# Attention and a gated product on one Trainium2 core: value rows issued from ScalarE's queue, queries of two groups by one set of transfers, a new written order

## The chip, the cores and the metric

The kernel runs on one core of one Trainium2 chip. The metric is device time in microseconds (us) of one execution, on that core.

The engines are named as the profile names them: PE (TensorE, matrix products), DVE (VectorE), ACT (ScalarE), POOL (GpSimd) and SP (SyncE, which here only issues transfers). SPq and ACTq are the queues of SP and ACT when they issue a transfer.

## What is computed

```python
# q, k, v: (4, 8, 768, 64); x: (3072, 512); w_a, w_b: (512, 1536); w_out: (1536, 512)
k_sum = k.reshape(B, H, nb, block, D).max(axis=3)       # block = 32
v_sum = v.reshape(B, H, nb, block, D).mean(axis=3)
mask_l = np.abs(pos[:, None] - pos[None, :]) < window    # window = 16
scores_s = scale * np.einsum('bhsd,bhnd->bhsn', q, k_sum) + np.log(block)
a = softmax over [masked local scores, scores_s]
attn = a @ concatenate([v, v_sum])                       # then (tokens, 512)
out = ((x @ w_a) * (x @ w_b)) @ w_out                    # x = attn
```

Each query sees the keys within 16 places and one summary of every block of 32 keys. What comes out of the attention is the input x of a gated product with three weights.

## The kernel before

**Tiles and stages.** The tokens are worked in groups of 128. A group is 8 heads of 128 queries; its scores have 120 columns (96 keys near it and 24 block summaries). Groups are put together in nine chunks: three chunks of two groups for batch 0, then two chunks of three groups for each of batches 1 to 3. For each chunk the gated product runs over 12 column blocks f of the weights: `up` (line 1055) multiplies the chunk's x by block f of w_a and w_b, ACT and DVE form the gated value (lines 1088 to 1096 for two groups, 1120 to 1128 for three), and `down` (line 1137) adds its product with block f of w_out to the output banks. The eight blocks f = 3 to 10 of the first two chunks are done together, so that their weights are needed only once early on.

**The start.** `first_attention` (line 850) works the first four groups (chunks 0 and 1). It loads six blocks of keys (line 491), which PE turns (line 436), ACT copies to the key tile kT (lines 495 and 496) and DVE reduces to block maxima (line 503). Queries of groups 0 to 3 come by four transfers to the tiles space_154 and space_163; PE turns them and ACT copies them to qT and space_161 (line 928). PE writes the masks (line 640) and the scores (line 653) to PSUM banks; DVE takes the maxima (line 690), ACT the exponentials (line 719, or 711 for a whole half), DVE the sums and reciprocals, POOL the division (line 745). PE turns the probabilities (line 758), ACT copies them (line 770) and PE multiplies them by the value rows (line 806). The block means of the values come from three more transfers of v (line 885), summed on DVE (line 889) and POOL (line 900).

**Value rows.** `load_values` (line 614) brings the value rows of one group by three transfers, 96 (or 80), 32 and 64 (or 48) rows of 8 heads, 2 KB a row. For the first four groups that is twelve transfers, to the tiles vw_133 and vw_134 (group 0), space_160 (group 1), space_165 and space_166 (groups 2 and 3). All of them are issued by SP.

**Queries of later chunks.** From the second batch on, `begin` (line 992) loads the queries of each group into one of two halves of the tile qin: 16 transfers of 32 rows for each group (`blocks`, line 438), the half taken in turn by the group's number (line 983).

**Weights.** `load_part` loads each of 36 parts of the weights (512 KB, line 375) into a tile raw_n. `convert` splits each part into a high and a low half: ACT line 400, DVE lines 403 and 411, ACT line 416, POOL line 419.

**What sets the order.** Every operation is given to `Work` with its engine, an estimated time and the keys that it reads and writes. `Work.emit` (line 89) issues them by rank and estimated readiness; for the first several hundred operations the table `ORDER` gives the order on each engine by operation number. Each engine then works its own list strictly from first to last.

**Semaphores of transfers.** The built program gives every transfer, whichever engine issues it, one of eight semaphores, DMAHW0 to DMAHW7, in turn, in the order in which the operations were emitted. The issuing instruction waits until the transfer that held the same semaphore before has landed. In the lists below `[waits DMAHW2_49]` is that wait, and the transfer which waits for a semaphore is also the next one to hold it.

Of the kernel before, what the change touches and what calls it, by code (L numbers as in the profile page):

```python
# [22 lines left out]

ORDER = {
# [5 lines left out]
    ],  # L30
    "ACT": [
# [6 lines left out]
    ],  # L38
    "DVE": [
# [6 lines left out]
    ],  # L46
    "POOL": [
        25, 46, 52, 81, 47, 53, 48, 54, 88, 49, 55, 191, 106, 100, 109, 114, 112, 108, 196,
        133, 206, 139, 211, 113, 222, 228, 159, 201, 166, 216, 110, 234, 240, 246, 264, 252,
        258, 270, 468, 304, 276, 316,  # L50
    ],
# [5 lines left out]
    ],  # L57
}

# [79 lines left out]
def attention_moe(  # L139
# [10 lines left out]
    nc = tc.nc  # L150
    B, H, S, D = q.shape
    P = 128
    DM = H * D
    FF = w_a.shape[1] // 2
    NP = H // 2
# [6 lines left out]
    CH = 256  # L162
    G = CH // P
# [3 lines left out]
    chunks = [(b, t, n) for b, n in enumerate((G, WIDE, WIDE, WIDE)) for t in range(0, S // P, n)]  # L167
# [69 lines left out]
    for base, sign in ((32, 1), (-31, -1)):  # L237
        nc.gpsimd.affine_select(
            out=pairs, in_=pairs, compare_op=ALU.is_ge, fill=0.0, base=base,
# [18 lines left out]
    qin = sb([P, NP, CH], "qin")  # L258
# [44 lines left out]
    def area(i):  # L303
        return spaces[f"P{i}"], [f"P{i}.0", f"P{i}.1"]

    x, MK = area(27)
    x = x.bitcast(F32R)
# [7 lines left out]
        out=maskr[1], in0=mask[:, :2, :], in1=maskr[0].bitcast(F32), op=ALU.subtract  # L315
# [15 lines left out]
    def pool(rank, takes, reads, writes, fn):  # L331
        work.add("POOL", rank, takes, 0.13, reads, writes, fn)

    def load(rank, kb, rate, reads, writes, out, in_):
        work.add(
            "SP", rank, 0.45, kb, reads, writes,
            lambda: nc.sync.dma_start(out=out, in_=in_), rate=rate,  # L337
        )


# [21 lines left out]
    def load_part(i, rank):  # L362
        f, nm = parts[i]
        w = {"a": w_a, "b": w_b, "o": w_out}[nm]
        if nm == "o":
            src = w[f * P : (f + 1) * P, :]
        else:
            src = w[:, 2 * f * P : 2 * (f + 1) * P].rearrange("(c p) n -> p c n", p=P)

        def fn():  # L370
            raws[i] = wp.tile([P, 1024], I32, tag=f"P{i}", name=f"raw{i}")
            dst = raws[i]
            if nm != "o":
                dst = dst.rearrange("p (c n) -> p c n", c=NP)
            nc.sync.dma_start(out=dst, in_=src)

        work.add(
            "SP", rank, 0.45, 524.0, (), [f"raw{i}", f"P{i}.0", f"P{i}.1"], fn, rate=375 if nm == "o" else 340
        )

    def convert(i):
# [49 lines left out]
    def heads(x):  # L431
        return x.rearrange("h p d -> p h d")
# [178 lines left out]
                    summed(b)[:, 4 * hg + h], y[h * NS : (h + 1) * NS],  # L611
                )

    def load_values(b, t, vw, keys, rank):
        row = t * P
        skip = 16 if t == 0 else 0
        end = min(row + P + 16, S)
        for i, (e, r0, lo, hi) in enumerate((
            (0, skip, row - 16 + skip, row + 80),
            (1, 0, row + 48, row + 80),  # L620
            (1, 32 + NS, row + 80, end),
        )):
            load(
                rank, 2.1 * (hi - lo), 170, (), [keys[i]], vw[e][r0 : r0 + hi - lo],
                heads(v[b, :, lo:hi, :]),
            )

    def scores(u, t, qT, qk, s, sk, banks, lead=None, way="AA"):
# [221 lines left out]
    def first_attention():  # L850
        first_keys()
        x, qk = area(19)
# [10 lines left out]
        x, key = area(26)  # L863
# [3 lines left out]
        x, key = area(24)  # L867
        s1 = [x[:, h * 512 : (h + 1) * 512].rearrange("p (c x) -> p c x", x=P) for h in range(2)]
        s, sk = [s0, s1], [SK, key]
        vws, vks = [vbuf], [VK]  # L870
        for a in (25, 30, 31):
            x, key = area(a)
# [5 lines left out]
        x, key = area(29)  # L878
# [4 lines left out]
        for n in range(3):  # L883
            x, key = area(20 + n)
            load(10 + n, 524.0, 375, (), key, x, halves[n * P : (n + 1) * P])
            if MEANS[n] == "D":
# [3 lines left out]
                        out=rows[:, n, :], in_=x.rearrange("p (t d) -> p d t", d=D),  # L890
# [3 lines left out]
            else:  # L894
                m = 512
                while m >= D:
                    out = x[:, :m] if m > D else rows[:, n, :]
# [3 lines left out]
                            out=out, in0=x[:, :m], in1=x[:, m : 2 * m], op=ALU.add  # L901
# [14 lines left out]

            pe(FIRST + 0.5, 0.4, [f"vr{n}"], ["h0"], means)
        for g in range(4):
            load_values(0, g, vws[g], vks[g][:3], (16, 18, 20.5, 20.7)[g])

        def begin(g, bk):
            u, i = g // G, g % G
# [44 lines left out]
    def attention(u):  # L967

        b, t0, n = chunks[u]
        rank = rank_of(u)  # L970
        banks, vbank = ["c0", "c1"], ["c0", "c1"] if u == FILL else ["o3"] * n
        if t0 == 0:
            prep_keys(b)
            prep_values(b)
        qk = []
        old = [f"qin.{c}.{r}" for c in range(NP) for r in range(0, P, 32)]
        if n == G:
            for c in range(NP):
                qk += blocks(
                    98, f"qin.{c}", qin[:, c, :], q, b, c, t0 * P, ["lo8"] if u == FILL else ()  # L980
                )

        def place(i):
            return slice((t0 + i) % 2 * P, ((t0 + i) % 2 + 1) * P)

        def bring(i):
            load_values(b, t0 + i, vbuf, VK[:3], 97)
            if t0 == 0 and i == 0:
                for e, r0 in ((0, WIN), (1, 32)):
                    load(89.5 if b == 1 else 97, 49.0, 100, VS + (["S1.3"] if b == 1 else []), [VK[3 + e]], vbuf[e][r0 : r0 + NS], summed(b))  # L990

        def begin(i):
            keys = list(qk)
            if n != G:
                for c in range(NP):
                    keys += blocks(
                        98, f"q{(t0 + i) % 2}.{c}", qin[:, c, place(i)], q, b, c, (t0 + i) * P, (),
                        old if chunks[u - 1][2] == G and i < 2 else (),
                    )
            dve(  # L1000
                rank_of(u, t0 + i) - 0.05 * (u > FILL), 0.62, keys, ["qT"],
                lambda: nc.vector.transpose(out=qTs, in_=qin[:, :, place(i)]),
            )
            scores(u, t0 + i, qTs, "qT", s0, SK, banks, lead=lead.pop() if lead else None)

        def turned(i):
            transposes(u, t0 + i, s0, SK, banks)

        def end(i):
            pt = (pown, [PU, ["S0.2", "S0.3"]]) if u == FILL and i else None  # L1010
            return u, t0 + i, vbuf, VK, vbank[i], pt

        if u == FILL:

            yield
            bring(0)
            begin(0)
            turned(0)
            yield
            begin(1)  # L1020
            pool(rank, 0.9, (), ["S0.2", "S0.3"], lambda: nc.gpsimd.memset(pown, 0.0))
            turned(1)
            yield
            values(*end(0))
            bring(1)
            values(*end(1))
        else:
            for i in range(n):
                begin(i)
                bring(i)  # L1030
                turned(i)
                if u == FILL + 1:
                    values(*end(i))
                else:
                    lead.append(products(*end(i)))
        if u == NU - 1:
            reads, bk, fn, split = lead.pop()
            pe(-1, 1.1, reads, [bk], fn)
            split()
        yield  # L1040
# [173 lines left out]
    for n, (us, f) in enumerate(items):  # L1214
        item(n, us, f)
        u = us[0]
# [36 lines left out]
```

## Time and profile before

| | us |
|---|---|
| median of 3 runs (658.92 to 660.45) | 660.11 |
| the profiled execution | 659.72 |
| its span, first to last instruction | 658.0 |
| PE busy | 639.9 (97%) |
| DVE busy | 398.5 (61%) |
| ACT busy | 242.0 (37%) |
| POOL busy | 155.9 (24%) |

Of the profiled execution 659.72 - 658.0 = 1.7 us lie around the span. The shares of busy time are averages: PE is waited for nearly everywhere after the first 36 us, the other engines mostly in the first 200 us. Idle time of an engine matters only where the work that ends last runs through it.

### The profile page before, as it was taken

Reading aid. Unit: us, or ns where it says so; the run is one execution under the profiler, and the core shown is the slowest. Engines: PE = TensorE matmul, PEld = TensorE weight load, DVE = VectorE, ACT = ScalarE, POOL = GpSimd, SP = SyncE. Lnnn points to the kernel's source line nnn. Section 1 sums busy time; section 2 is a strip of 40 time slices with the busy share of each in tenths; the row PEclk is TensorE's granted clock in tenths of the full one; section 3 lists DMA queues with packets and bytes.
Section 4 is the critical chain, followed back from the end, with each engine's and each line's share of the span. In section 5 each row is a group of like instructions: output and inputs, shape, how many; then the busy total and the mean of one; then the engine's idle time right before and its main releaser. Section 6 shows DMA issues by size and latency. Waiting matters only on the chain.

```text
span 658.0 us, 12911 instructions
## 1 busy us (share of the span) xinstructions
PE 639.9 (97%) x4908; PEld 591.9 (90%) x4908; DVE 398.5 (61%) x866; ACT 242.0 (37%) x695; POOL 155.9 (24%) x238
## 2 busy tenths in 40 slices
PE   6799999999999999999999999999999999999997
PEld 4599887899888999999999999999999999999996
DVE  3886899986686785566776864676664531122212
ACT  3896787323333331233334312343331411121111
POOL 5873657423233222122322100111110100000000
PEclk9799999999999999999999999999999999999999
DMA  9999983632333234422223222122110200010001
GB/s 241 276 286 264 345 203 68 117 103 49 67 76 90 54 68 84 106 55 61 42 65 89 53 41 50 30 78 41 26 25 0 72 1 0 1 49 0 1 1 48
DMA packets 154645, 54.70 MB, mean 83 GB/s; under 512 B 134728, under 2 KB 147272, under 8 KB 154584
## 3 DMA queue, kind: packets, MB, share of 16 engines
q1 hardware_dynamic: 154440, 53.75, 34.0%
q8 instruction: 38, 0.62, 0.4%
q14 instruction: 23, 0.19, 0.1%
q10 hardware_dynamic: 144, 0.13, 0.1%
HBM read 47.12 MB, written 6.29 MB: 81 GB/s over the span
## 4 chain that ended last, share of the span: by engine, by line
PE 84%; DVE 9%; SPq 2%; issue 2%; DMA 1%; ACT 1%; DVEq 0%; ACTq 0%
PE h L1055 49%; PE o L1137 26%; PE o L806 3%; PE c L653 3%; SPq L337 2%; DVE c L403 2%; DVE pt L790 2%; DVE S L411 1%; DMA space<-in_k_dram 1%; PE o L640 1%; PE o L758 1%; DVE nml L690 1%; DVE s L682 0%; PE o L653 0%; DVE h L1123 0%
## 5 line engine op out<-in xcount | busy, mean ns | idle before, releaser
L1055 PE MATMUL h<-x,w 128*128 128x384 f32 (+2 forms) x2100 | 390.1, 319 | 0.0
L1055 PEld LDWEIGHTS h<-x,w 128*128 128x128 f32 x2100 | 334.5, 190 | 9.2 <-issue 0.3
L1137 PE MATMUL o<-w,gh 128*128 128x512 f32 x731 | 176.1, 382 | 0.0
L1137 PEld LDWEIGHTS o<-w,gh 128*128 128x128 f32 x731 | 134.3, 189 | 18.2 <-issue 2.7
L1123 DVE TENSOR_TENSOR h<-h,g 128x384 f32<-128x384 f32 (+1 forms) x79 | 45.8, 579 | 139.8 <-PE h L1055 139.6
L1125 ACT CAST gh<-h 128x384 fp32r<-128x384 f32 x71 | 34.0, 478 | 216.4 <-DVE h L1123 214.8
L790 DVE STREAM_TRANSPOSE pt<-s 32x256 f32<-32x256 f32 x228 | 99.3, 435 | 12.6 <-POOL s L745 8.9
L745 POOL TENSOR_TENSOR s<-s,nml 128x480 f32<-128x480 f32 x44 | 43.4, 987 | 215.6 <-DVE nml L741 140.7
L1055 PE MATMUL h<-late,w 128*128 128x384 f32 x288 | 94.0, 326 | 0.3 <-DVE late L829 0.3
L719 ACT ACTIVATE s<-s,nml 128x120 f32<-128x120 f32 x160 | 61.3, 386 | 33.6 <-DVE nml L690 32.9
L1120 ACT COPY g<-h 128x384 f32<-128x384 f32 (+1 forms) x80 | 39.3, 491 | 59.9 <-PE h L1055 58.9
L1055 PEld LDWEIGHTS h<-late,w 128*128 128x128 f32 x288 | 54.4, 189 | 1.6 <-DVE late L829 0.6
L1128 DVE TENSOR_TENSOR gh<-h,gh 128x384 fp32r<-128x384 f32 x71 | 39.3, 554 | 20.8 <-ACT gh L1125 19.9
L577 POOL TENSOR_TENSOR S<-S 96x256 f32<-96x256 f32 (+3 forms) x58 | 33.1, 571 | 56.9 <-DMA S<-in_v_dram 53.9
L682 DVE SCALAR_TENSOR_TENSOR s<-c,mask 128x480 f32<-128x480 f32 x40 | 26.0, 652 | 23.6 <-PE c L653 23.3
L1137 PE MATMUL o<-w,x 128*128 128x512 f32 x133 | 32.9, 385 | 1.0 <-ACT x L1125 1.0
L419 POOL TENSOR_TENSOR w<-S,w 128x512 fp32r<-128x512 f32 x24 | 30.4, 1284 | 11.4 <-ACT w L416 10.2
L403 DVE TENSOR_SCALAR c<-raw 128x512 int32<-128x512 uint32 x36 | 28.4, 801 | 3.8 <-DMA raw<-in_moe_w_b_dram 2.7
L719 ACT ACTIVATION_READ_ACCUMULATOR s<-s,nml 128x1 f32 x160 | 30.2, 189 | 0.0
L1137 PEld LDWEIGHTS o<-w,x 128*128 128x128 f32 x133 | 24.1, 189 | 5.1 <-ACT x L1125 1.6
L690 DVE TENSOR_REDUCE nml<-s 128x4 f32<-128x480 f32 x40 | 25.8, 647 | 0.6
L806 PEld LDWEIGHTS o<-pt,vw 120*64 120x64 f32 x576 | 18.5, 138 | 6.6 <-issue 3.1
(133 smaller groups left out, 450.1 us busy)
## 6 DMA issues: line engine op xcount, KB each, us to landing
raw<-in_moe_w_a_dram SPq DMA_DIRECT2D x12, 512.0 KB
raw<-in_moe_w_b_dram SPq DMA_DIRECT2D x12, 512.0 KB
raw<-in_moe_w_out_dram SPq DMA_DIRECT2D x12, 512.0 KB
out_dram<-S SPq DMA_DIRECT2D x23, 256.0 KB
qin<-in_q_dram SPq DMA_DIRECT2D x288, 16.0 KB
S<-in_v_dram SPq DMA_DIRECT2D x24, 192.0 KB
kin<-in_k_dram SPq DMA_DIRECT2D x38, 100.0 KB
vw<-in_v_dram SPq DMA_DIRECT2D x17, 192.0 KB
```

Source lines behind the costliest of these rows:

```text
L403: dve(rank, 0.66, [raw], [bk], lambda: nc.vector.tensor_scalar(out=z.bitcast(I32), in0=word(0).bitcast(U32), scalar1=2.0**-29, scalar2=7.0 ...
L577: lambda: nc.gpsimd.tensor_tensor(out=out, in0=i0, in1=i1, op=ALU.add),
L719: lambda h=h, c=c, more=more: nc.scalar.activation(y[h][:, c, :], x[h][:, c, :], AF.Exp, bias=m[:, 0, h, c : c + 1], scale=1.0, **more,),
L745: lambda h=h, r=r: nc.gpsimd.tensor_tensor(out=y[h], in0=y[h], in1=r[:, :, None].broadcast_to([P, NP, COLS]), op=ALU.mult,),
L790: lambda js=js, qs=qs, rs=rs: nc.vector.transpose(out=pv[js, rs, qs], in_=sv[qs, rs, js]),
L806: nc.tensor.matmul(ps[h * D : (h + 1) * D, c, es], vw[e][:COLS, 2 * c + h, :], d[:COLS, h, c, es], start=True, stop=True, tile_position=(0 ...
L1055: nc.tensor.matmul(ps, w[:, c, part, :], xs[xpart][:, :, c].rearrange("p g (a b) -> p g b a", a=2), start=(i == 0), stop=(i == n - 1),)
L1120: act(CHAIN, 0.13 + W / 1030, ["h0"], gk, lambda: nc.scalar.copy(out=g, in_=pa))
L1123: lambda: nc.vector.tensor_tensor(out=pb, in0=pb, in1=g, op=ALU.mult),
L1125: act(CHAIN, 0.16 + W / 1030, [bk], ghks, lambda: nc.scalar.copy(out=gh, in_=pb))
L1128: lambda: nc.vector.tensor_tensor(out=gl, in0=pb, in1=gh.bitcast(F32), op=ALU.subtract),
L1137: nc.tensor.matmul(bank[ok[j]], (gh if first else gl)[:, j * P : (j + 1) * P], w[:, :, part, :].rearrange("p (z a) n -> p z n a", a=2), st ...
```

## The change

It has four parts.

1. The twelve value transfers of the first four groups are issued from ACT's queue, early, and no longer from SP's. Their estimated cost of issue in the planner is 0.4 us.
2. The queries of groups 0 and 1 of a chunk of three come by one set of 16 transfers into the whole of qin (32 x 8 x 32 elements each); group 2 has a set of its own, into half 0. The halves are taken by the group's place in its chunk.
3. A load of a weight part now waits in the planner for all the keys under which a tile's earlier contents are known.
4. `ORDER` is written anew for all engines, and is somewhat longer.

```diff
 ORDER = {
     "PE": [
-        17, 13, 21, 1, 71, 9, 5, 69, 91, 89, 72, 92, 115, 44, 122, 117, 50, 56, 124, 125,
...
+        21, 5, 17, 1, 9, 13, 69, 71, 72, 89, 91, 92, 44, 115, 50, 122, 117, 56, 124, 125,
...
-    def load(rank, kb, rate, reads, writes, out, in_):
+    def load(rank, kb, rate, reads, writes, out, in_, queue="SP"):
+        eng = {"SP": nc.sync, "ACT": nc.scalar}[queue]
         work.add(
-            "SP", rank, 0.45, kb, reads, writes,
-            lambda: nc.sync.dma_start(out=out, in_=in_), rate=rate,
+            queue, rank, 0.47 if queue == "SP" else 0.4, kb, reads, writes,
+            lambda: eng.dma_start(out=out, in_=in_), rate=rate,
         )
...
+        keys = [f"P{i}.{z}{x}" for z in range(2) for x in ("", "b", "s", *range(NP))]
         work.add(
-            "SP", rank, 0.45, 524.0, (), [f"raw{i}", f"P{i}.0", f"P{i}.1"], fn, rate=375 if nm == "o" else 340
+            "SP", rank, 0.47, 524.0, (), [f"raw{i}", *keys], fn, rate=375 if nm == "o" else 340
         )
...
-    def load_values(b, t, vw, keys, rank):
+    def load_values(b, t, vw, keys, rank, queue="SP"):
...
         for g in range(4):
-            load_values(0, g, vws[g], vks[g][:3], (16, 18, 20.5, 20.7)[g])
+            load_values(0, g, vws[g], vks[g][:3], (0.5, 0.9, 1.5, 2)[g], "ACT")
...
         def place(i):
-            return slice((t0 + i) % 2 * P, ((t0 + i) % 2 + 1) * P)
+            return slice(i % 2 * P, (i % 2 + 1) * P)
...
         def begin(i):
             keys = list(qk)
+            if n != G and i != 1:
+                z = slice(0, CH) if i == 0 else place(i)
+                for c in range(NP):
+                    also = [f"q1.{c}.{r}" for r in range(0, P, 32)] if i == 0 else []
+                    also += old if i == 0 and chunks[u - 1][2] == G else []
+                    blocks(98, f"q0.{c}", qin[:, c, z], q, b, c, (t0 + i) * P, (), also)
             if n != G:
-                for c in range(NP):
-                    keys += blocks(
-                        98, f"q{(t0 + i) % 2}.{c}", qin[:, c, place(i)], q, b, c, (t0 + i) * P, (),
-                        old if chunks[u - 1][2] == G and i < 2 else (),
-                    )
+                keys += [f"q{i % 2}.{c}.{r}" for c in range(NP) for r in range(0, P, 32)]
```

Lines of the changed kernel stand 5 lower near lines 436 to 806 and 7 lower near 1055: 495 is 500 there, 653 is 658, 719 is 724, 1055 is 1062.

**ACT, the start.** This is ACT's list of the kernel before, from the second block of keys up to the conversion of the first weight part. The tiles c_77, c_78, o_73, o_74 and h_76 are PSUM banks; qT and space_161 take the queries of groups 0 and 1.

```order
L495 COPY kT<-c_77 128x4x80 [waits PE_49]
L496 COPY kT<-c_77 128x4x48
L495 COPY kT<-o_74 128x4x80 [waits DVE_49]
L496 COPY kT<-o_74 128x4x48
L495 COPY kT<-o_73 128x4x80 [waits PE_49]
L496 COPY kT<-o_73 128x4x48
L495 COPY kT<-c_78 128x4x80 [waits DVE_49]
L496 COPY kT<-c_78 128x4x48
L928 ACTIVATE qT<-c_77 128x512 [waits PE_49]
L928 ACTIVATE space_161<-c_78 128x512 [waits PE_49]
L495 COPY kT<-h_76 128x4x80
L496 COPY kT<-h_76 128x4x48
```

There is no transfer in it. In the changed kernel one block of keys is copied, then come six value transfers, two more blocks and a seventh; the list then goes on as follows, up to the copy of group 1's queries.

```order
L500 COPY kT<-c_77 128x4x80 [waits DVE_49]
L501 COPY kT<-c_77 128x4x48
L341 DMA space_166<-in_v_dram 96x8x64 [waits DMAHW2_49]
L341 DMA space_166<-in_v_dram 64x8x64 [waits DMAHW4_49]
L341 DMA space_165<-in_v_dram 96x8x64 [waits DMAHW6_49]
L933 ACTIVATE qT<-c_77 128x512 [waits PE_49]
L500 COPY kT<-o_73 128x4x80 [waits DVE_49]
L501 COPY kT<-o_73 128x4x48
L341 DMA space_165<-in_v_dram 64x8x64 [waits DMAHW7_49]
L500 COPY kT<-o_74 128x4x80 [waits DVE_49]
L501 COPY kT<-o_74 128x4x48
L341 DMA space_166<-in_v_dram 32x8x64 [waits DMAHW0_49]
```

Five value transfers now stand between the key copies and ahead of the copies of both queries; the copy of group 1's queries (line 933, space_161) is the next row.

**SP, the start.** These are the transfers of the kernel before that follow the six of keys; raw is a weight part, in_q, in_k and in_v are the inputs in memory.

```order
L337 DMA space_154<-in_q_dram 128x8x64 x2
L375 DMA raw_206<-in_moe_w_a_dram 128x4x256 [waits DMAHW0_49]
L337 DMA space_156<-in_v_dram 128x1024 [waits DMAHW1_49]
L337 DMA space_157<-in_v_dram 128x1024 [waits DMAHW2_49]
L337 DMA space_155<-in_v_dram 128x1024 [waits DMAHW3_49]
L375 DMA raw_215<-in_moe_w_b_dram 128x4x256 [waits DMAHW4_49]
L337 DMA space_163<-in_q_dram 128x8x64 [waits DMAHW5_49]
L375 DMA raw_225<-in_moe_w_out_dram 128x1024 [waits DMAHW6_49]
L375 DMA raw_227<-in_moe_w_a_dram 128x4x256 [waits DMAHW7_49]
L337 DMA space_160<-in_v_dram 32x8x64 [waits DMAHW0_49]
```

And these are those of the changed kernel, from the second transfer of queries on.

```order
L341 DMA space_154<-in_q_dram 128x8x64 [waits DMAHW0_49]
L341 DMA space_155<-in_v_dram 128x1024 [waits DMAHW2_49]
L341 DMA space_157<-in_v_dram 128x1024 [waits DMAHW4_49]
L379 DMA raw_217<-in_moe_w_a_dram 128x4x256 [waits DMAHW6_49]
L341 DMA space_163<-in_q_dram 128x8x64 [waits DMAHW0_49]
L379 DMA raw_222<-in_moe_w_b_dram 128x4x256 [waits DMAHW2_49]
L379 DMA raw_229<-in_moe_w_a_dram 128x4x256 [waits DMAHW4_49]
L341 DMA space_163<-in_q_dram 128x8x64 [waits DMAHW6_49]
L379 DMA raw_241<-in_moe_w_out_dram 128x1024 [waits DMAHW7_49]
L379 DMA raw_247<-in_moe_w_out_dram 128x1024 [waits DMAHW0_49]
```

The semaphores that SP's list skips are held by ACT's transfers. Read together with ACT's list, ACT's five waits there (DMAHW2, 4, 6, 7 and 0, in this order) are for the last transfers shown here that hold these semaphores: raw_222, raw_229, the second space_163, raw_241 and raw_247.

**SP, the second batch.** These rows of the kernel before bring the first queries of the second batch, after the last weight part.

```order
L337 DMA vw_133<-in_v_dram 96x8x64
L337 DMA vw_134<-in_v_dram 32x8x64
L337 DMA kin<-in_k_dram 32x25x32 x4
L337 DMA qin<-in_q_dram 32x4x32 x23
L337 DMA S_149<-in_v_dram 96x512
L337 DMA qin<-in_q_dram 32x4x32 x2
```

In the changed kernel one set stands there.

```order
L341 DMA S_149<-in_k_dram 32x25x32 x4
L341 DMA qin<-in_q_dram 32x8x32 x16
L341 DMA kin<-in_k_dram 32x25x32 x4
L341 DMA S_149<-in_v_dram 96x512 x2
L341 DMA kin<-in_k_dram 32x25x32 x4
```

Two sets of 16 transfers of one group each have become one set of 16 for two groups, and it stands ahead of the keys.

More of the change, by code (lines that the diff above doesn't have):

```diff
@@ L25 @@
     "PE": [
[4 rows of a table removed]
[4 rows of a table added]
     ],
     "ACT": [
[6 rows of a table removed]
[8 rows of a table added]
     ],
     "DVE": [
[6 rows of a table removed]
[7 rows of a table added]
     ],
     "POOL": [
-        25, 46, 52, 81, 47, 53, 48, 54, 88, 49, 55, 191, 106, 100, 109, 114, 112, 108, 196,
-        133, 206, 139, 211, 113, 222, 228, 159, 201, 166, 216, 110, 234, 240, 246, 264, 252,
-        258, 270, 468, 304, 276, 316,
[3 rows of a table added]
     ],
     "SP": [
[4 rows of a table removed]
[4 rows of a table added]
     ],
@@ L623, in load_values @@
             load(
-                rank, 2.1 * (hi - lo), 170, (), [keys[i]], vw[e][r0 : r0 + hi - lo],
-                heads(v[b, :, lo:hi, :]),
+                rank, 2.1 * (hi - lo), 170 if queue == "SP" else 200, (), [keys[i]],
+                vw[e][r0 : r0 + hi - lo], heads(v[b, :, lo:hi, :]), queue,
             )
```

44 rows, old and new, of the table ORDER are left out of this document.

## The prediction, made before the changed kernel had run

> **What bounds the kernel now.** I read the page first, then the chain of work that ended last, then PE's timeline. The page's shares and PE's busy tenths in 40 slices of 16.45 us:
>
> ```profile
> PE 639.9 (97%) x4908; PEld 591.9 (90%) x4908; DVE 398.5 (61%) x866; ACT 242.0 (37%) x695; POOL 155.9 (24%) x238
> PE   6799999999999999999999999999999999999997
> ```
>
> PE is the engine that sets the time, except in the first two slices and the last. The chain (start us, us, what) says where those lose it:
>
> ```profile
> 3.82 5.16 DMA space<-in_k_dram
> 9.03 1.12 PE c L436 x4
> ...
> 12.70 0.23 ACT kT L496
> ...
> 36.30 2.72 PE h L1055 x24
> ...
> 649.59 3.96 PE o L1137 x18
> ```
>
> It begins with the transfers of keys, runs through the attention of the first groups, and from 36.30 us it is PE's product nearly to the end. PE's timeline shows the idle time ahead of a row in brackets:
>
> ```profile
> 5.43 1.08 PE L436 MATMUL h<-ident,space 128*128 128x128 f32 x4 [5.43 <-DMA space<-in_k_dram]
> ...
> 36.08 2.94 PE L1055 MATMUL h<-x,w 128*128 128x256 f32 x24
> ...
> 105.08 1.99 PE L1137 MATMUL o<-w,x 128*128 128x512 f32 x8 [0.99 <-ACT x L1125]
> ...
> 165.47 0.34 PE L806 MATMUL o<-pt,vw 120*64 120x64 f32 x4 [1.28 <-DVE s L682]
> 166.21 1.03 PE L806 MATMUL o<-pt,vw 120*64 120x64 f32 x28 [0.41 <-DVE h L1091]
> ...
> 199.79 0.43 PE L1055 MATMUL h<-late,w 128*128 128x384 f32 x1 [0.30 <-DVE late L829]
> ```
>
> Between 36.08 and 199.79 us its waits are 0.99 + 1.28 + 0.41 + 0.30 = 2.98 us, and later I find none that matters. So the time is the moment at which the first product of line 1055 starts, plus a stretch of PE work that the change leaves as it is, plus at most 3 us. Whatever moves that start by x moves the end by x, less what is won back of the 3 us.
>
> **The value rows on ACT's queue.** ACT is not busy in the first 16 us, but its work there is on the way to the start of PE's product. Its timeline before:
>
> ```profile
> 6.56 0.42 ACT L495 COPY kT<-h 128x320 f32<-128x320 f32 x1 [4.46 <-PE h L436]
> 10.18 0.43 ACT L495 COPY kT<-c 128x320 f32<-128x320 f32 x1 [2.98 <-PE c L436]
> 14.27 0.43 ACT L495 COPY kT<-c 128x320 f32<-128x320 f32 x1 [1.35 <-DVE ksum L503]
> 15.67 0.60 ACT L928 ACTIVATE space<-c 128x512 f32<-128x512 f32 x1 [0.24 <-PE c L436]
> 17.34 0.36 ACT L719 ACTIVATE s<-o,nml 128x120 f32<-128x120 f32 x1
> 19.01 0.36 ACT L719 ACTIVATE s<-o,nml 128x120 f32<-128x120 f32 x1
> ```
>
> The queries of group 1 are copied by 15.67 + 0.60 = 16.27 us; the first exponential follows at 17.34. The cheap reading of the change is that twelve issues fit into ACT's gaps. One issue that nothing holds up takes 0.43 us (the least of a form), so twelve are 5.2 us, beside gaps of 4.46 + 2.98 + 1.35 + 0.24 = 9.0 us:
>
> ```profile
> L337 SPq DMA_DIRECT2D space<-in_v_dram x7: 430/962/1884, 9.7 to 29.0; - x7
> ```
>
> But an issue waits for the transfer that held its semaphore before, and what stands behind it on its engine waits too. SP shows this between 48 and 64 us (waited for: us in total, times, longest), where it issues in order and stands still until earlier weights have landed:
>
> ```profile
> SPq L337 <- DMA raw<-in_moe_w_b_dram: 2.5, 2, 1.3
> SPq L337 <- DMA raw<-in_moe_w_a_dram: 1.4, 2, 1.0
> ```
>
> The Trainium skill ("DMA: Bandwidth & Descriptors", section "Anatomy of one DMA") says that the transfer engines never wait on semaphores and that a wait sits on the issuing sequencer; SP's rows agree.
>
> On SP nobody stands behind such a wait but other transfers. On ACT, by the changed order, the five transfers ahead of the copy of group 1's queries wait for raw_222, raw_229, the second space_163, raw_241 and raw_247 to land. raw_247 is the second w_out part, and nearly all other early data are issued ahead of it. How long that takes I read from what moved before. Sizes (KB each):
>
> ```profile
> raw<-in_moe_w_a_dram SPq DMA_DIRECT2D x12, 512.0 KB
> space<-in_k_dram SPq DMA_DIRECT2D x6, 256.0 KB
> space<-in_v_dram SPq DMA_DIRECT2D x3, 512.0 KB
> vw<-in_v_dram SPq DMA_DIRECT2D x2, 160.0 KB
> ```
>
> The last is the 80 rows of group 0: 2 KB a row. Landed with raw_247 are six blocks of keys (1536 KB), four of queries of the same shape (1024), three of v (1536), five weight parts (2560) and all value rows but the last 32 (176 + 3 x 192 - 32 = 720 rows, 1440 KB): 8096 KB, 8.29 MB. The stretches of before (last two columns: share of the DMA engines, GB/s):
>
> ```profile
> 0.00:10.00 10.00, 4.29 (x17) 3.12 (x18) 2.33 (x5) 1.93 (x3) 8.02 (x40) 1.00 1.02 177
> 10.00:20.00 10.00, 6.76 (x89) 5.13 (x88) 6.85 (x14) 7.17 (x26) 3.37 (x6) 1.00 1.14 335
> 20.00:30.00 10.00, 8.35 (x70) 6.05 (x71) 7.58 (x17) 7.65 (x16) 8.93 (x13) 0.66 0.99 226
> 30.00:40.00 10.00, 10.00 (x151) 8.91 (x150) 10.00 (x21) 9.06 (x20) 7.66 (x9) 1.00 1.18 289
> ```
>
> The engines of the transfers are full (0.99 to 1.18), and 1.77 + 3.35 + 2.26 = 7.38 MB have moved by 30 us; the other 0.91 MB at 289 GB/s end at 33.1 us. The rate of 20 to 30 us may be the price of value rows in small pieces between weights; if the 335 GB/s of the stretch ahead held on, 8.29 MB would be there at 10 + (8.29 - 1.77) / 0.335 = 29.5 us. I take 32.0, nearer to what these transfers took before. Then one issue (0.43) and the copy (0.60): group 1's queries are ready at 33.0 us (30.5 to 34.1) and no longer at 16.27. Group 0's copy stands behind the second space_163 and is late as well, so that PE and DVE, which take their lists in order, have nothing to go past it.
>
> **From there to the first product of line 1055.** Behind group 1's copy ACT's new list has, up to the second cast of x that this product needs, 8 exponentials, 3 first conversions, 4 half exponentials, 4 copies of probabilities, 2 of queries, 2 of means, 3 casts of weights and 2 of x. Its groups of 0 to 40 us (busy us, mean ns):
>
> ```profile
> L400 ACT ACTIVATE space<-raw 128x512 f32<-128x512 f32 x4 | 2.9, 713 | 0.0
> L416 ACT CAST w<-space 128x512 fp32r<-128x512 f32 x3 | 2.0, 655 | 0.0
> L770 ACT COPY pt<-o 120x512 f32<-120x512 f32 x3 | 1.8, 608 | 0.7 <-DVE c L403 0.6
> L825 ACT CAST x<-h 128x512 fp32r<-128x512 f32 x2 | 1.2, 588 | 0.0
> L711 ACT ACTIVATE s<-s 128x480 f32<-128x480 f32 x2 | 1.2, 604 | 0.2 <-DVE s L704 0.2
> L947 ACT COPY vw<-h 24x512 f32<-24x512 f32 x2 | 1.2, 579 | 0.4 <-PE h L911 0.4
> ```
>
> An exponential with its sum takes (19.01 - 17.34) / 4 = 0.42. The sum: 8 x 0.42 + 3 x 0.71 + 4 x 0.60 + 4 x 0.61 + 2 x 0.60 + 2 x 0.58 + 3 x 0.66 + 2 x 0.59 = 15.8 us. Neighbours overlap a little and POOL and PE are waited for a little; I let these cancel. DVE's low half of x comes last:
>
> ```profile
> 35.34 0.67 DVE L829 TENSOR_TENSOR x<-h,x 128x512 fp32r<-128x512 f32 x1
> ```
>
> The first product then starts at 33.0 + 15.8 + 0.7 = 49.5 us in place of 36.08: 13.4 us later (10.9 to 14.5 by the ends above). Before, the same way took 36.08 - 16.27 = 19.8 us, with waits for values, weights and half the clock (0.66 granted in 20 to 30 us); by then all of these have landed, which is why I take less.
>
> **The queries of two groups at once.** Of each chunk of three, 48 issues become 32. The chain of 140 to 166 us runs through SP's issues of queries and ends in the stalls of 1.28 and 0.41 us:
>
> ```profile
> 147.34 1.60 SPq L337
> ...
> 155.25 1.48 DMA qin<-in_q_dram
> 156.73 0.70 DVE qT L1002
> ```
>
> With one set, issued ahead of the keys, I let both stalls go: -1.7 us (0 if DVE, busy through that stretch, is late anyway; -2.98 if all waits go). What it costs: group 0 of the next chunk now takes the place that the last group of a chunk has just left, so its transfers cannot come early. PE's product covers that, and I cost it at nothing (the fourth rival has its price). The planner's added keys only order transfers that are far apart.
>
> **The sum.** 659.72 + 13.4 - 1.7 = 671.4 us on the profiled execution's footing; the median of the runs was 0.4 above it, so I say 671.8. By the bounds: 659.7 + 10.9 - 3.0 = 667.6 to 659.7 + 14.5 + 0.4 = 674.6.
>
> **Rivals.** *The data come sooner* (0.13). Two queues side by side may fill what one leaves empty. The best stretch above moves 335 GB/s; were it 410 from 10 us on, raw_247 would land at 25.9, the start be 43.4, and the time 659.7 + 7.3 - 1.7 = 665.3, or 664 with all waits gone. For it: the low 226 GB/s. Against it: the engines' share is already 0.99 there.
>
> *Faster* (0.05). If ACT is never held, the new order helps the start. The first block that PE turns is now the first that is issued; blocks land (8.98 - 5.43) / 3 = 1.2 us apart, so PE begins 1.2 us earlier, and with the -1.7 the time is 657. It decides by one point: raw_247 would have to be there when ACT, unheld, reaches its row, at about 5.4 + 6 x 0.66 + 12 x 0.43 + 2 x 0.60 = 15.7 us (0.66 being the two pieces of a block, 0.43 and the 0.23 of the chain). By 20 us only 5.1 of the 8.29 MB had moved. Only a misreading of the semaphores would save it.
>
> *No change* (0.03). The start is late, but PE's product may in truth be paced by the conversion of weights up to the wait at 105 us, and swallow it: 660 to 661. For it: that wait of 0.99. Against it: PE's rows have no holes; 24 products of 256 columns take 2.72 us at 36 us, so there is no room for 13 us. The Trainium skill, same page, section "Issuing engines are not separate DMA queues", comes to no change in another way: a second issuing engine saves only sequencer time. By that rule alone the twelve issues move off SP and nothing else happens; it leaves out who stands behind a waiting issue.
>
> *The query slot too* (0.08). Sixteen issues of 0.43, 1.48 of landing and 0.70 of turning are 9.1 us from a free half to the next group's queries. If 1 us of it shows on PE at each of five chunk changes, the time is 677.
>
> **Chances.** My forecast has 0.71. The range runs from the first rival's lower half to the fourth: 665 to 677. A measurement of this kernel can tell about 0.2% (1.3 us) from no change; slower by more has 0.71 + 0.13 + 0.08 = 0.92, faster 0.05, the same 0.03.
>
> **What would show it.** Right: ACT's timeline has long gaps ahead of its value transfers and of lines 933 and 501, ended by transfers of weights; the scores of group 0 (line 658) start near 28 us and those of group 1 near 33, where before the first exponential behind them came at 17.34; the first row of line 1062 starts between 47 and 50.5; PE is dense behind it; the stall at 165 is gone. Wrong: line 933's second copy is done by 20 us, or the first product starts before 40, or PE has new waits of several us behind 50 us.

## The result, and the profile after

The changed kernel takes 669.15 us (median of four runs, 668.91 to 669.44); the kernel before takes 659.79 beside it (four runs, 658.92 to 660.45). The ratio is 1.0145, with a 95% interval of 1.013 to 1.0161: slower, as predicted, and 2.65 us below the predicted 671.8. The profiled execution took 668.98 us, with a span of 667.3.

The page's shares and PE's busy tenths. PE is as busy as before, but the first three slices are emptier:

```profile
PE 639.7 (96%) x4908; PEld 593.2 (89%) x4908; DVE 398.8 (60%) x866; ACT 241.5 (36%) x695; POOL 156.2 (23%) x238
PE   3489999999999999999999999999999999999997
```

ACT's timeline shows why. A row of `ACTq` with a count is several issues in a row, and its length holds the waits between them; a row of a single issue begins when its wait is over:

```profile
14.53 1.33 ACTq L341 DMA_DIRECT2D space<-in_v_dram  x1
15.91 0.43 ACT L500 COPY kT<-c 128x320 f32<-128x320 f32 x1 [9.93 <-issue]
...
24.19 3.77 ACTq L341 DMA_DIRECT2D space<-in_v_dram  x3
28.01 0.60 ACT L933 ACTIVATE qT<-c 128x512 f32<-128x512 f32 x1 [8.11 <-DMA space<-in_q_dram]
...
28.70 1.34 ACTq L341 DMA_DIRECT2D space<-in_v_dram  x1
...
30.38 1.77 ACTq L341 DMA_DIRECT2D space<-in_v_dram  x1
32.20 0.60 ACT L933 ACTIVATE space<-c 128x512 f32<-128x512 f32 x1 [1.46 <-PE c L441]
```

The second block of keys is copied at 15.91 us after a gap of 9.93, the queries of group 0 at 28.01 after one of 8.11, and those of group 1 are ready at 32.20 + 0.60 = 32.80 us, against 16.27 before. The chain of work that ended last leads through the second of these waits:

```profile
12.09 7.77 DMA raw<-in_moe_w_a_dram
19.88 7.52 DMA space<-in_q_dram
27.42 0.53 ACTq L341
28.01 0.60 ACT qT L933
...
30.53 1.06 PE c L441 x4
31.59 0.60 issue
```

It reads: a weight part is issued at 12.09 and lands at 19.86; SP, which waited for its semaphore, issues the second space_163 at 19.88; that lands at 27.40; ACT, which waited for that one's semaphore, issues a value transfer at 27.42, and only then copies the queries of group 0. PE works the scores of group 0 and turns the queries of group 1 up to 31.59; ACT copies those at 32.20, when its last value issue (30.38 + 1.77 = 32.15) is through.

PE's timeline: the scores of the two groups (line 658), the first product (line 1062), and the last row with idle time ahead of it up to 600 us:

```profile
28.66 1.88 PE L658 MATMUL o<-kT,qT 64*64 64x120 f32 x32 [5.88 <-ACT qT L933]
...
32.95 1.05 PE L658 MATMUL o<-kT,space 64*64 64x120 f32 x32
...
48.68 2.94 PE L1062 MATMUL h<-x,w 128*128 128x256 f32 x24
51.99 1.09 PE L763 MATMUL o<-ident,s 128*120 128x128 f32 x8 [0.36 <-POOL s L750]
```

The first product is 48.68 - 36.08 = 12.6 us later, and the span is 667.3 - 658.0 = 9.3 us longer. The 3.3 us between them are found in PE's stretch from the first product to the end. The view by stretches gives its length and PE's busy time, of before:

```profile
36.08:659.00 622.92, 614.44 (x4623) 1.00 0.30 73
```

and of the changed kernel:

```profile
48.68:668.00 619.32, 613.77 (x4628) 1.00 0.27 66
```

Up to the end of the span, PE is idle for 621.92 - 614.44 = 7.48 us before and 618.62 - 613.77 = 4.85 us after. So 2.63 us of idle time are gone, and 0.67 us of busy time: 12.60 - 2.63 - 0.67 = 9.30.

Data moved faster than I had allowed (the last column is GB/s):

```profile
10.00:20.00 10.00, 2.02 (x9) 1.62 (x9) 2.75 (x5) 1.85 (x6) 0.61 (x4) 1.00 1.17 309
20.00:30.00 10.00, 4.12 (x36) 3.20 (x40) 0.00 (x0) 1.14 (x3) 4.36 (x5) 1.00 1.14 308
30.00:40.00 10.00, 7.32 (x84) 5.28 (x76) 8.50 (x19) 7.68 (x26) 4.09 (x7) 1.00 1.14 300
```

The 226 GB/s of 20 to 30 us are gone.

### The profile page after: what moved, and what is told of

Its sections match the earlier page's. It is cut to its first block, busy times and chain, and to the rows that moved or that the text cites. A ratio compares the mean times of both kernels' runs of the same rounds, so it can differ in the third digit from the quotient of the medians.

```text
span 667.3 us, 12786 instructions
## 1 busy us (share of the span) xinstructions
PE 639.7 (96%) x4908; PEld 593.2 (89%) x4908; DVE 398.8 (60%) x866; ACT 241.5 (36%) x695; POOL 156.2 (23%) x238
## 4 chain that ended last, share of the span: by engine, by line
PE 92%; DMA 3%; POOL 1%; DVE 1%; SPq 1%; issue 1%; ACT 0%; ACTq 0%; POOLq 0%
PE h L1062 56%; PE o L1144 29%; PE o L811 3%; PE c L658 3%; DMA space<-in_q_dram 2%; DMA raw<-in_moe_w_a_dram 1%; SPq L341 1%; POOL w L424 0%; POOL space L959 0%; PE c L811 0%; PE o L763 0%; POOL s L750 0%; PE c L1062 0%; PE o L658 0%; ACT s L724 0%
```

## The experiments

Theory A is that of the prediction: ACT is held by the landing of whatever held the semaphore before, and the copies that stand behind the held issue set the start of PE's product. Against it stand that the issues themselves cost the time, that late value data do, and, for the other part of the change, that the joint query sets win nothing; each expectation names the rivals that it weighs. The line numbers in the rows are each kernel's own. 57 to 68 are the numbers of the twelve value transfers in `ORDER`, 90 is the copy of group 1's queries.

### All value rows back on SP, the rest of the change kept

```diff
-            load_values(0, g, vws[g], vks[g][:3], (0.5, 0.9, 1.5, 2)[g], "ACT")
+            load_values(0, g, vws[g], vks[g][:3], (16, 18, 20.5, 20.7)[g])
...
     "ACT": [
-        22, 61, 58, 59, 60, 57, 62, 6, 18, 64, 2, 66, 68, 63, 70, 10, 65, 14, 67, 90, 76,
+        22, 6, 18, 2, 70, 10, 14, 90, 76, 78, 75, 77, 85, 82, 84, 83, 187, 102, 116, 96,
...
     "SP": [
-        20, 0, 4, 16, 12, 8, 38, 45, 39, 42, 51, 181, 40, 182, 184, 41, 183, 186, 185, 217,
+        20, 0, 4, 16, 12, 8, 38, 45, 39, 42, 51, 181, 40, 182, 184, 61, 60, 57, 58, 59,
```

> The changed kernel with its twelve value transfers issued by SP again, at the places that the list of before gave them; new order and joint query sets stay. Theory (ACT is held by the semaphore waits of its transfers): group 1's queries are copied before 18 us, the first product of line 1062 starts at 34 to 36.5, the waits of PE between 100 and 200 us stay gone, 655 to 658 us. Rival (the new order itself is slow at the start): the first product stays at 45 or later, 666 us or more.

Measured: 655.40 us (median of six, 654.69 to 658.47), beside 659.12 of before (seventeen runs); ratio 0.9943 (0.9926 to 0.996). This beats both kernels. ACT and PE:

```profile
14.82 0.60 ACT L931 ACTIVATE space<-c 128x512 f32<-128x512 f32 x1 [0.81 <-PE c L439]
```

```profile
32.24 2.94 PE L1060 MATMUL h<-x,w 128*128 128x256 f32 x24
```

ACT is held by nothing, group 1's queries are ready at 15.42, and the product starts at 32.24 us: 3.8 earlier than before, 16.4 earlier than in the changed kernel. So the value rows on ACT cost 669.15 - 655.40 = 13.75 us (13.3 by the two ratios, which take each set's own kernel before), and the rest of the change wins 659.12 - 655.40 = 3.7.

### Only the value rows on ACT, in the kernel before

`load`, `load_part` and `load_values` as in the change, the orders of before, with the twelve taken out of SP's list and this list of ACT, in which the copy of group 0's queries (70) also stands ahead of the last key copy (6):

```diff
     "ACT": [
-        18, 2, 14, 10, 6, 70, 90, 22, 187, 77, 76, 75, 78, 82, 83, 84, 96, 102, 85, 116,
+        18, 61, 58, 59, 60, 57, 62, 2, 14, 64, 10, 66, 68, 63, 70, 6, 65, 67, 90, 22,
```

> The kernel before with only the value transfers moved to ACT, at like places in its list; order of the other engines and the queries' transfers as before. The last of them waits here for raw6, a weight part later than in the changed kernel. Theory (held by waits): ACT's copy of group 1's queries ends near 36 us, the first product starts at 50 to 53, 673 to 677 us, since the stalls later stay in part. Rival (the new order itself): 659 to 661. Rival (only the twelve issues of 0.3 to 0.5 us cost): first product near 41, 664 to 665.

Measured: 681.51 us (680.8 to 682.75), ratio 1.0335 (1.032 to 1.035): slower, and by more than expected. ACT and PE:

```profile
32.11 2.94 ACTq L336 DMA_DIRECT2D space<-in_v_dram  x1
...
35.09 2.17 ACTq L336 DMA_DIRECT2D space<-in_v_dram  x1
37.31 0.60 ACT L928 ACTIVATE space<-c 128x512 f32<-128x512 f32 x1 [4.14 <-issue]
```

```profile
57.45 2.94 PE L1055 MATMUL h<-x,w 128*128 128x256 f32 x24
```

The last two issues ahead of the copy of group 1's queries are 2.94 and 2.17 us long. The second of them waited for nothing: in the trace the transfer that held its semaphore had landed at 33.47 us, 1.6 us before the row begins. So the copy stood behind the length of an issue here, not behind a landing, and the copy ended at 37.91 where 36 was expected. The way from there to the product is 19.5 us long, as in the kernel before (19.8), although the transfers that ACT had waited for had landed by then. That is told against the prediction below.

### Only the joint query sets, in the kernel before

`place` and `begin` as in the change; nothing else.

> The kernel before with only the joint transfers of queries. First product at 36.1 as before. Theory A (the sets win back the 3.3 us): the stalls of 1.28 and 0.41 us at 165 are gone, 656.5 to 658.3. Theory B (they were won back because weights and conversions are further ahead of a late start, or by the new order): 659.3 to 660.3.

Measured: 659.11 us (657.45 to 661.39, eleven runs), ratio 0.9995 (0.9983 to 1.0008): no change. PE's rows from the first product to 230 us that have idle time, and the first product:

```profile
35.29 2.94 PE L1057 MATMUL h<-x,w 128*128 128x256 f32 x24
...
104.37 1.99 PE L1139 MATMUL o<-w,x 128*128 128x512 f32 x8 [1.07 <-ACT x L1127]
164.15 1.04 PE L806 MATMUL o<-pt,vw 120*64 120x64 f32 x28 [0.41 <-DVE pt L790]
175.08 1.67 PE L1139 MATMUL o<-w,gh 128*128 128x512 f32 x6 [0.34 <-ACT gh L1095]
198.48 0.43 PE L1057 MATMUL h<-late,w 128*128 128x384 f32 x1 [0.30 <-DVE late L829]
```

The stall of 1.28 us is gone, that of 0.41 stays, and one of 0.34 appears. What the profile shows as won, 0.9 us, is not seen in the times: the sets alone win back nothing of the 3.3 us.

### Only the new order

The changed kernel with the value rows on SP (the edit of the first experiment) and with `place` and `begin` of before.

> The changed kernel without both transfers' changes: value rows on SP, query sets of one group as before; only the new order is left. Theory (held by waits) with A: first product at 34 to 36.5, some stall near 165 back, 657 to 660. With B by the order: 655 to 657.5. Rival (the new order itself is slow): 666 or more.

Measured: 657.38 us (656.04 to 658.4, five runs), ratio 0.996 (0.9947 to 0.9973). PE:

```profile
32.94 2.94 PE L1058 MATMUL h<-x,w 128*128 128x256 f32 x24
...
70.28 2.86 PE L1058 MATMUL h<-x,w 128*128 128x512 f32 x12 [0.91 <-ACT g L1123]
165.19 0.34 PE L809 MATMUL o<-pt,vw 120*64 120x64 f32 x4 [0.64 <-DVE nml L693]
165.96 1.04 PE L809 MATMUL o<-pt,vw 120*64 120x64 f32 x28 [0.43 <-DMA vw<-S]
```

The order alone starts the product 3.1 us earlier and is 0.4% faster. Its waits at 70 and 165 us, 0.91 + 0.64 + 0.43 = 1.98 us, are not there in the first experiment, which has the joint sets too and is 657.38 - 655.40 = 1.98 us faster. That the two figures agree to the hundredth is chance: the profiled executions differ by 656.7 - 654.4 = 2.3 us of span, of which 0.7 us is the start, which the sets do not touch. The two intervals of the times overlap, and 657.38 lies in the range of both theories. So it is the profile of one execution each, not the times, that says that the sets help in the new order.

### Two groups of four on ACT

```diff
-            load_values(0, g, vws[g], vks[g][:3], (0.5, 0.9, 1.5, 2)[g], "ACT")
+            load_values(0, g, vws[g], vks[g][:3], (0.5, 0.9, 20.5, 20.7)[g], "ACT" if g < 2 else "SP")
...
     "ACT": [
-        22, 61, 58, 59, 60, 57, 62, 6, 18, 64, 2, 66, 68, 63, 70, 10, 65, 14, 67, 90, 76,
+        22, 61, 58, 59, 60, 57, 62, 6, 18, 2, 70, 10, 14, 90, 76, 78, 75, 77, 85, 82,
```

> The changed kernel with the value rows of groups 2 and 3 (six transfers) back on SP; the six of groups 0 and 1 stay on ACT, ahead of the second block of keys. Theory A (ACT is held by the landing of what held the semaphore before): the six wait only for blocks of keys and for the first v transfer, which landed by 13.5 us, and for no weight. ACT's last issue then ends between 14 and 16 us; five pairs of key copies and two query copies put the copy of group 1's queries at 20 to 25 us, the first product at 37 to 41, the time at 660 to 664 us. Theory C (the issues themselves, or value rows that move early beside the weights, cost the time): half of the transfers stay, so about half of the 13.7 us between all on SP (655.4) and all on ACT (669.15): the same 660 to 664, but with the copy at 15 to 16 us. The two are told apart by ACT's gaps, not by the time.

Measured: 663.62 us (661.57 to 663.76), ratio 1.0061 (1.0042 to 1.008). ACT and PE:

```profile
14.51 1.51 ACTq L340 DMA_DIRECT2D space<-in_v_dram  x1
16.06 0.42 ACT L499 COPY kT<-c 128x320 f32<-128x320 f32 x1 [9.97 <-issue]
...
23.76 0.60 ACT L932 ACTIVATE space<-c 128x512 f32<-128x512 f32 x1 [1.60 <-PE c L440]
```

```profile
42.20 2.94 PE L1061 MATMUL h<-x,w 128*128 128x256 f32 x24
```

The first gap is that of the changed kernel (9.97 against 9.93), the later ones are gone, and the copy is at 23.76 as theory A has it, not at 15 to 16 as C. The product starts 1.2 us later than my range. In the trace the six issues wait for blocks of keys and one transfer of v, the last of which lands at 13.53 us, and for no weight; the last issue then takes 1.51 us. So these six, which the prediction's sum leaves out, are enough for 663.62 - 655.40 = 8.2 us.

### All twelve at the head of ACT's list

```diff
     "ACT": [
-        22, 61, 58, 59, 60, 57, 62, 6, 18, 64, 2, 66, 68, 63, 70, 10, 65, 14, 67, 90, 76,
+        61, 58, 59, 60, 57, 62, 64, 66, 68, 63, 65, 67, 22, 6, 18, 2, 70, 10, 14, 90,
```

> The changed kernel with all twelve value transfers at the very head of ACT's list, ahead of the first key copy. They wait for blocks of keys and for each other, for no weight and no query. Same twelve issues on ACT, same bytes, earlier. Theory A: the last issue ends at 11 to 14 us, behind it the key copies; 1.44 MB of values at 300 GB/s push the keys back by up to 5 us; the copy of group 1's queries ends at 19 to 22 us and the first product starts at 35.5 to 39, the time 658 to 662 us. Theory C (twelve issues on ACT cost what they cost wherever they stand, or the values disturb the weights): 665 to 670 us.

Measured: 664.27 us (662.84 to 664.49), ratio 1.0077 (1.0059 to 1.0095): between the two theories. ACT, then PE:

```profile
6.18 9.34 ACTq L340 DMA_DIRECT2D space<-in_v_dram  x7
...
26.04 0.60 ACT L932 ACTIVATE space<-c 128x512 f32<-128x512 f32 x1 [2.54 <-PE c L440]
```

```profile
14.32 1.97 PE L440 MATMUL o<-ident,space 128*128 128x128 f32 x8 [2.11 <-DMA space<-in_k_dram]
...
42.55 2.94 PE L1061 MATMUL h<-x,w 128*128 128x256 f32 x24
```

Seven issues are spread over 9.34 us, though they wait for no weight: in the trace each of the seven begins 0.02 us after an earlier value transfer has landed. ACT's first key copy comes at 16.85 us, against 5.37 with the values on SP; 1.28 us of this is the load of a table (ACT_TABLE_LOAD), which stands behind all twelve issues here and at 0.81 us there. And the last two blocks of keys are turned at 14.32 us, against 10.20 with the values on SP. So it need not be a weight that is waited for: value rows that hold each other up, and that move ahead of keys, cost 664.27 - 655.40 = 8.9 us, the table's load included.

### One transfer of 64 KB on ACT, and the same one at the head of the list

From the kernel of the first experiment, only the 32 rows of group 3 (67) go to ACT. They are needed last of all. In the first of the two kernels they stand just ahead of the copy of group 1's queries, in the second at the head:

```diff
+            if late:
+                queue = "ACT" if i == 1 else "SP"
...
     "ACT": [
-        22, 6, 18, 2, 70, 10, 14, 90, 76, 78, 75, 77, 85, 82, 84, 83, 187, 102, 116, 96,
+        22, 6, 18, 2, 70, 10, 14, 67, 90, 76, 78, 75, 77, 85, 82, 84, 83, 187, 102, 116,
```

> The version with all value rows on SP (655.40 us), with one transfer of the twelve (32 rows of group 3, 64 KB, needed last) on ACT, right ahead of the copy of group 1's queries. The turn of the semaphores is the same as there, and its predecessor is the 48- or 64-row transfer of group 0, which landed at 26.0 us. Theory A: ACT stands still from 14.5 to 26.0 us; the copy of group 1's queries, 14.82 there, starts at 26.4, 11.6 later; the stretch behind it may be up to 3 us shorter, since all data have landed; first product at 41 to 44 in place of 32.24, time 664 to 667 us. Theory C (the issue itself costs): 0.4 us, 655.4 to 656. Theory D (late value data): none, 655.4.

> The kernel of the previous experiment with its one value transfer on ACT moved from just ahead of the copy of group 1's queries to the head of ACT's list. It is then among the first eight transfers of the program, its semaphore is fresh and it waits for nothing; the turn of the semaphores moves by one on SP. The other eleven are on SP as before. Theory A (only the wait costs, for what stands behind it): the copy of group 1's queries is back at 15 to 16 us, the first product at 32 to 33.5, the time 655 to 657 us, with 0.2 us for 64 KB ahead of the keys. Theory C (an issue on ACT costs by itself): 664 again, as with the same issue later in the list.

Measured, just ahead of the copy: 664.62 us (663.52 to 665.23), ratio 1.0079 (1.0062 to 1.0096). At the head: 656.38 us (655.79 to 656.93), ratio 0.9957 (0.9943 to 0.9971). ACT and PE of the first:

```profile
26.11 0.41 ACTq L340 DMA_DIRECT2D space<-in_v_dram  x1
26.57 0.60 ACT L934 ACTIVATE space<-c 128x512 f32<-128x512 f32 x1 [11.82 <-DMA vw<-in_v_dram]
```

```profile
44.13 2.05 PE L1063 MATMUL h<-x,w 128*128 128x256 f32 x16
```

and of the second:

```profile
0.81 0.46 ACTq L340 DMA_DIRECT2D space<-in_v_dram  x1
...
15.32 0.60 ACT L934 ACTIVATE space<-c 128x512 f32<-128x512 f32 x1 [0.81 <-PE c L440]
```

```profile
32.47 2.94 PE L1063 MATMUL h<-x,w 128*128 128x256 f32 x24
```

The same issue of the same 64 KB on the same engine costs 8.2 us more in one place than in the other. In the one it waits 11.8 us for a value transfer that SP issued; in the other it waits for nothing. C falls for this transfer (its issue takes 0.41 and 0.46 us), and so does D (nobody needs these rows until later). C does not fall for every issue: taken one by one, the twelve on ACT are 0.32 to 1.77 us long in the changed kernel, 8.5 us in sum, and up to 2.94 us in the old order.

### Group 0's three transfers at the head of ACT's list

The kernel of the first experiment with 58, 59 and 57 at the head of ACT's list, the other nine on SP.

> The version with all value rows on SP (655.40 us), with the three transfers of group 0 (176 rows, 352 KB) at the head of ACT's list, where none of them waits for another transfer. SP then has three issues less between 18.7 and 23.7 us. Theory A: ACT is held by nothing but a clearing of the tile at about 1 us; 352 KB at 300 GB/s push the keys back by up to 1.2 us, and weights may come up to 1.2 us sooner behind them; first product at 31.5 to 33.5, time 654.5 to 657 us. Rival (value rows that move among the first blocks of keys cost what they cost in the kernel with all twelve first): three of twelve, a quarter of 8.9 us, 657 to 658 us.

Measured: 655.48 us (654.76 to 656.24), ratio 0.9946 (0.9931 to 0.996): as good as with all on SP. But the product starts later, outside my range. PE's rows of this kernel:

```profile
34.66 2.95 PE L1061 MATMUL h<-x,w 128*128 128x256 f32 x24
...
50.37 2.84 PE L1061 MATMUL h<-x,w 128*128 128x256 f32 x24
```

and with all on SP:

```profile
41.62 2.94 PE L1060 MATMUL h<-x,w 128*128 128x256 f32 x24 [0.45 <-DVE gh L1101]
...
46.13 1.13 PE L1142 MATMUL o<-w,gh 128*128 128x512 f32 x4 [0.24 <-DVE x L832]
...
50.40 2.84 PE L1060 MATMUL h<-x,w 128*128 128x256 f32 x24
```

One starts 2.4 us later than the other, and at 50.4 us they are level: the earlier start is given away in small waits for what ACT and DVE convert and multiply.

### The runs side by side

The kernel before, run beside each of the three sets of experiments, took 659.12, 658.96 and 659.4 us.

| kernel | first product, us | span, us | span less start | median, us |
|---|---|---|---|---|
| before | 36.08 | 658.0 | 621.9 | 659.79 |
| changed | 48.68 | 667.3 | 618.6 | 669.15 |
| all values on SP | 32.24 | 654.4 | 622.2 | 655.40 |
| only values on ACT | 57.45 | 681.0 | 623.6 | 681.51 |
| only joint query sets | 35.29 | 656.7 | 621.4 | 659.11 |
| only the new order | 32.94 | 656.7 | 623.8 | 657.38 |
| two groups on ACT | 42.20 | 660.9 | 618.7 | 663.62 |
| all twelve first | 42.55 | 661.1 | 618.6 | 664.27 |
| one transfer, late | 44.13 | 662.9 | 618.8 | 664.62 |
| one transfer, at the head | 32.47 | 654.1 | 621.6 | 656.38 |
| group 0 at the head | 34.66 | 653.6 | 618.9 | 655.48 |

With the new order and the joint sets, the span is the start plus 618.6 to 618.9 us for every start from 34.66 to 48.68. An earlier start than that brings nothing more.

## Why the prediction was right, point by point

**The end moves with the start of the first product.** Right in this range: the table shows it over 14 us. It fails on the early side, below some 34 us, which the changed kernel does not reach.

**ACT waits for five landings.** Right as to the waits: in the trace each of the five issues begins when the transfer named for it has landed, the chain shows the one for the second space_163, and the single 64 KB transfer shows the price of one. But two terms were off. raw_247 had landed when ACT's last issue began, at 30.38 us and not at 32.0: I leaned to the rate of before in 20 to 30 us (226 GB/s), and 308 came. And that issue took 1.77 us where my sum had 0.43, the least of its form. That the copy was nevertheless ready when I said (32.80 against 33.0) is luck: a landing 1.6 us early and an issue 1.3 us long. (The view puts the copy's idle 1.46 us down to PE, whose turning of group 1's queries, behind the late scores of group 0, ended at 31.59; the issue ended at 32.15.) Nor are the five the whole of it: the six issues ahead of them hold ACT for 9.93 us, and with two groups on ACT such six cost 8.2 us without the five.

**From the copy to the product.** I said 16.5 us, and it is 48.68 - 32.80 = 15.9. The number came out of ACT's new list and holds. The reason that I gave for taking less than the 19.8 us of before, that the data had landed, fails: in the old order with the values on ACT the transfers that ACT waited for had landed too, and the way took 19.5. In the new order it took 32.24 - 15.42 = 16.8 with the data still coming. Over all runs it is 18.6 to 19.8 us in the three kernels of the old order and 15.9 to 17.8 in the eight of the new one. So it is the new order that shortens it. PE's clock was granted at half in some of these stretches, for instance in the old order with the values on ACT

```profile
37.91:47.91 10.00, 6.50 (x56) 4.79 (x57) 8.00 (x16) 8.06 (x26) 5.81 (x9) 0.50 1.16 285
```

and with one late transfer in the new order,

```profile
27.17:35.17 8.00, 7.36 (x64) 5.58 (x64) 6.23 (x18) 7.01 (x23) 4.08 (x7) 0.50 1.05 339
```

where the way was 17.0 us, 1.1 more than the changed kernel's. At nearly the same clock, 0.85 and then 0.81 in the kernel before and 0.79 and then 0.82 with two groups on ACT, the way was 19.8 and 17.8. So some 2 us belong to the new order; the rest may be the clock's or the data's, and is not separated.

**The joint query sets win 1.7 us.** The step that failed: "With one set, issued ahead of the keys, I let both stalls go". All 2.98 us of the waits went, as the upper end had it, but not by the sets: alone they bring nothing that the times show (0.9995, 0.9983 to 1.0008). The order removes the waits at 105 and 199 us and makes others, and these are not there with the sets in the new order.

**The sum.** Against 671.4 on the profiled execution's footing stand 668.98: 0.8 us less of late start (12.6 for 13.4) and 1.6 more won back (3.3 for 1.7).

**The rivals.** *The data come sooner* was half true: raw_247 was there 1.6 us before my value, and not at 25.9. *Faster* did not come, since its condition, raw_247 there by 15.7 us, was missed by far. What it says of ACT not held is right, as the values on SP show, but its price was too small: the order brings the start 3.1 us forward by itself and 3.8 with the sets, not 1.2, and the time to 655.4, not 657. *No change*: the product did not swallow the late start. *The query slot too*: PE has no such wait at a chunk change.

**What stays open.** PE's busy time behind the first product is 0.67 us shorter than before, with 4628 records of matrix products for 4623; nothing shows why. How much of a stretch's length the clock sets is not measured. What makes one issue on ACT 0.3 us long and another 2.9 is not known, and so it is open how the 13.75 us divide between waits for landings and the length of the issues. The third part of the change, the planner's keys for weight parts, was never run by itself.

## What to carry to other kernels

A transfer that is issued from a compute engine is an instruction of that engine: ask which transfer held its semaphore before, when that one lands, and what stands behind the issue in the engine's list. The issue itself can be long too (0.3 to 2.9 us here). Put such issues where their semaphore is surely free (here the first eight transfers of the program), or leave them with an engine that has nothing else to do. When an edit comes with a new order, time the two apart: here one won 3.7 us, and the other lost 13.7.

## What the runs showed of the hardware

With the value rows issued from ACT between the weights of SP, the early data moved at 308 and 300 GB/s in 20 to 40 us, against 226 and 289 before. This goes with the move to ACT and not with the written order: 277 and 313 GB/s in the old order with the values on ACT, 238 and 262 in the new order with them on SP. With all twelve first, 10 to 20 us moved 226. The Trainium skill ("DMA: Bandwidth & Descriptors", section "Issuing engines are not separate DMA queues") says that a second issuing engine saves only sequencer time; no run here separates the second queue from the values' changed places among the transfers.

In the changed kernel the clock's column reads 1.00 throughout, yet 32 score products took 1.88 us at 28.66, behind 5.88 us without work on PE, and 1.05 us at 32.95. So PE was slow there for a moment, and the column did not show it. The Trainium skill ("TensorE: Matmul & The Clock Gate", section "What's actually happening") says that PE runs at half its clock by default and is released by some 3.4 us of work; these rows fit that.
